# Other loads for the decay columns, and a new order for the first eight stages of a fused linear-attention and MLP kernel

## The chip, the cores and the metric

The kernel runs on one core of a Trainium2 chip. The metric is device time in microseconds (us) of one execution, and the kernel before has a median of 165.37 us over three runs (165.07 to 165.39). The engines are PE (TensorE), DVE (VectorE), ACT (ScalarE), POOL (GpSimd) and SP (SyncE). Each has its own instruction stream, runs it in order, and waits on semaphores. SP, ACT and POOL also issue DMAs, each on queues of its own: in the profile q1 carries SP's loads, q10 those of ACT, and q0 those of POOL.

## The reference, cut to what matters

Four batches, eight heads, 768 tokens, head size 48. Per token and head the output is the query times the state plus a bonus for the token itself, and the state then decays by `w` and takes in the new key and value. The result, 3072 tokens by 384, goes through two matrices with a leaky ReLU between them.

```python
for t in range(S):
    kt, vt, rt = k[:, :, t], v[:, :, t], r[:, :, t]
    cur = einsum('bhd,bhe->bhde', u[None] * kt, vt)
    y[:, :, t] = einsum('bhd,bhde->bhe', rt, state + cur)
    state = w[None, :, :, None] * state + einsum('bhd,bhe->bhde', kt, vt)
x = y.transpose(0, 2, 1, 3).reshape(3072, 384)
h = x @ w_in                      # 384 -> 2048
out = maximum(0.01 * h, h) @ w_out  # 2048 -> 384
```

## The kernel before, in words

The 768 tokens of a batch are cut into 6 chunks of 128, which makes 24 stages. In a stage, tables of powers of `w` scale r and k (`prep`, written P; P5.0 is the half with r of stage 5, P5.1 the half with k). PE turns the products so that the head dimension lies on partitions (`turn`, T), ACT copies them from PSUM to SBUF, and PE forms the 128 by 128 score blocks (`a_mm`, A). DVE masks these into `at` (`a_mask`, M), multiplies the turned halves for the bonus (`diag`, X, into `prod`), and scales v by the bonus (`prep2`, Q, into `vs`). PE forms the bonus sums and the state's new part (`kv_mm`, K), DVE updates the state (`state`, S), and PE sums the stage's output from `at`, `st` and `vs` (`y_part`, Y), which ACT copies to `xT`. Then come the first matrix (`g1` for one stage, G; `g1_pair` for two stages, J) and the second (`g2`, H; `g2_seven`, N).

Stages 0 to 7 turn on PE; later ones by DMA transposes. A planner does not decide the order. A string of step names, `ORDER`, is walked from left to right, and each step appends its instructions to the streams of its engines; waits follow from what each reads and writes. So the string sets the order on all engines at once, up to about 60 us of the run. Behind it a plain loop emits the remaining pairs of stages. A second string, `LOADS`, sets the order of POOL's first instructions, most of them DMA issues: `t` is a column of token numbers (iota), `tri` the causal mask, `id` the identity, `wi0` a quarter of the first matrix, `r3` r of stage 3.

r and k of stages 0 and 1 do not come through POOL: SP issues those of r, ACT those of k, behind the small rows of `w` and `u`. `decay_columns` (C) brings `w` and `w*u` from a row on one partition to columns, head by head, by matmuls with one output column each. Their results feed `wcol` (ACT, logarithm) and `wu` (DVE), and through them the decay table `wl` (`decay_table`, W) and the bonus sums of K. `fill` (F) is a matmul of ones with ones whose result nobody reads.

```python
FIRST, EARLY = 8, 2
add("sp", lambda: SP.dma_start(w_row[:, :], row(w)), W=["w_row"], dma="w")
```

Of the kernel before, what the change touches and what calls it, by code (L numbers as in the profile page):

```python
# [16 lines left out]
HD = H * D  # L17
E = 64
# [106 lines left out]
def bass_rwkv5_eagle__then__act_leaky_relu_kernel(  # L125
# [49 lines left out]
    wu_row = SB("wu_row", [1, HD])  # L175
# [127 lines left out]
    for name in LOADS.split():  # L303
# [16 lines left out]
    add("dve", lambda: V.tensor_tensor(wu_row[:, :], w_row[:, :], u_row[:, :], ALU.mult),  # L320
        R=["w_row", "u_row"], W=["wu_row"])
# [7 lines left out]
    add("dve", lambda: V.memset(wu[:, :, :], 0.0), W=["wu"])  # L329
    fill(EARLY)  # L330
# [89 lines left out]
    def turn(n, *halves):  # L420
        it, iq = n % NTP, n % NQK
        for half in halves or ((0, 1) if n == 0 else (1, 0)):
            ps_t, key = next_bank()

            def emit(half=half, ps_t=ps_t):
                for p in range(NP):
                    h0 = half * H + 2 * p
                    last = PE.matmul(ps_t[:, 128 * p:128 * p + 128],  # L428
                                     qk[iq][:, h0:h0 + 2, :].rearrange("p h e -> p (h e)"), ident[:, :],
                                     start=True, stop=True)  # L430
# [4 lines left out]
            add("act", lambda dst=dst, ps_t=ps_t: A.activation(dst, ps_t[:, :], AF.Copy),  # L435
                R=[key], W=[("tp", it, half)])
# [51 lines left out]
    def a_mask(n, *parts):  # L488
# [9 lines left out]
        for hh in parts or range(2):  # L498
            part = at_bank[n][hh][0][:, :].rearrange("p (m i) -> p m i", i=128)
            add("dve", lambda hh=hh, part=part: V.tensor_tensor(  # L500
                at[n % NAT][:, hh, :, :], part, mask[:, :].unsqueeze(1).to_broadcast([128, NP, 128]), ALU.mult),
                R=[at_bank[n][hh][1], "mask"], W=[("at", n % NAT, hh)])
# [30 lines left out]
    def decay_columns():  # L533
        ps_c, key_c = next_bank()

        def emit():
            for hh in range(2):
                for p in range(NP):
                    c0 = (2 * p + hh) * D
                    rows = slice(64 * hh, 64 * hh + D)  # L540
                    PE.matmul(ps_c[rows, p:p + 1], w_row[:, c0:c0 + D], one_row[:, 0:1], start=True, stop=True)
                    last = PE.matmul(ps_c[rows, NP + p:NP + p + 1], wu_row[:, c0:c0 + D], one_row16[:, 0:1],
                                     start=True, stop=True)
            return last

        add("pe", emit, R=["one_row", "one_row16", "w_row", "wu_row"], W=[key_c, "wcols"])
# [322 lines left out]
    steps = {"U": u_table, "V": u_cast, "P": prep, "Q": prep2, "B": bonuses, "O": g_sum, "N": lambda m, *step: g2_seven(m, step=step[0] if step else None), "b": skip_banks, "I": g2_store, "t": swapped_tables, "m": swapped_mask, "E": lambda n, *heads: diag_tile(n, heads or range(H)), "D": lambda n: diag_tile(n, None), "T": turn, "A": a_mm, "M": a_mask, "K": kv_mm, "R": carry, "S": state, "Y": y_part, "X": diag, "C": decay_columns, "W": decay_table, "w": load_wout, "F": fill, "Z": w_sum,  # L869
# [116 lines left out]
```

## Time and profile before

| what | value |
|---|---|
| median of three runs | 165.37 us |
| the profiled execution | 165.09 us |
| its span (first to last instruction) | 163.4 us |
| PE busy in the span | 156.3 us (96%) |
| DVE, ACT, POOL busy | 124.4, 126.4, 79.1 us |
| loads from memory | 20.45 MB read, 4.72 MB written |

The span is what the trace shows; the execution's own time has 1.7 us more around it. A busy PE may still run slowly: the duration of a matmul of known size tells its rate, and the busy share does not. In the tables of groups and in the timeline the columns are the start, the time, the engine, the line of the kernel, the operation, and output and inputs; a wait, with what ended it, stands in brackets at the end.

### The profile page before, as it was taken

The page shows a single profiled execution, that of the slowest core. Times are in us where ns is not written, and L with a number is a line of the kernel's source. Part 1 is how long each engine was busy: PE and PEld are TensorE (multiplying, and loading weights), DVE is VectorE, ACT ScalarE, POOL GpSimd, SP SyncE. Part 2 cuts the span into 40 slices and gives each one's busy share as a digit, 9 for nine tenths or more (in the row PEclk, how much of TensorE's full clock was granted, in tenths as well). Part 3 has the DMA queues.
Part 4 walks back from the last instruction along what each step waited for, and adds up shares of the span by engine and source line. Part 5 has one row for each costly group of instructions (what it writes and reads, how often), then busy time and mean ns, then how long its engine had stood idle before and what let it go on. Part 6 is the DMA issues. An engine that isn't in the chain of part 4 may idle for free.

```text
span 163.4 us, 5788 instructions
## 1 busy us (share of the span) xinstructions
PE 156.3 (96%) x2444; PEld 135.4 (83%) x2444; DVE 124.4 (76%) x264; ACT 126.4 (77%) x313; POOL 79.1 (48%) x106
## 2 busy tenths in 40 slices
PE   5688999999999999999999999999999999999993
PEld 3557888788667889889889899899898899898993
DVE  7498997859999299997988988689889467055353
ACT  3565889879467989999999989989899827829430
POOL 7999992999936991780870961910000000000000
PEclk9999999999999999999999999999999999999999
DMA  5999999999999999999999996998209103003033
GB/s 107 161 172 184 157 155 173 202 188 139 140 118 177 169 204 127 179 105 93 192 105 95 186 110 118 178 85 153 72 4 194 35 4 96 0 18 84 4 96 98
DMA packets 99710, 19.91 MB, mean 122 GB/s; under 512 B 92770, under 2 KB 99684, under 8 KB 99684
## 3 DMA queue, kind: packets, MB, share of 16 engines
q0 software_dynamic: 74768, 9.84, 93.8%
q1 hardware_dynamic: 22836, 9.31, 29.4%
q10 hardware_dynamic: 2080, 0.39, 1.3%
q8 instruction: 19, 0.31, 0.8%
q14 instruction: 7, 0.06, 0.1%
HBM read 20.45 MB, written 4.72 MB: 154 GB/s over the span
## 4 chain that ended last, share of the span: by engine, by line
PE 90%; DVE 4%; DMA 4%; SPq 1%; issue 1%; DVEq 0%
PE ps_all L647 38%; PE ps_all L741 29%; PE ps_all L602 7%; PE ps_all L664 6%; DMA out_sb<-in_r_dram 4%; PE ps_all L516 2%; PE ps_all L469 2%; PE ps_all L451 2%; PE ps_all L428 2%; DVE at L500 2%; DVE qk L367 1%; DVE vs L383 1%; PE ps_all L630 0%; PE ps_all L512 0%; DVE st L567 0%
## 5 line engine op out<-in xcount | busy, mean ns | idle before, releaser
L647 PE MATMUL ps_all<-xT,w_in_sb 128*128 128x256 bf16 x564 | 65.0, 273 | 0.0
L647 PEld LDWEIGHTS ps_all<-xT,w_in_sb 128*128 128x128 bf16 x564 | 54.3, 98 | 6.5
L653 ACT ACTIVATE gT<-ps_all 128x512 bf16<-128x512 f32 x94 | 52.5, 596 | 3.5 <-PE ps_all L647 1.2
L416 ACT ACTIVATE at<-ident,s_tok 128x128 bf16<-128x128 bf16 x120 | 38.2, 392 | 0.3 <-DVE s_tok L397 0.3
L238 POOL DMA_DIRECT2D rk_sb<-in_k_dram x15 | 13.9, 925 | 19.4 <-PE ps_all L647 19.4
L741 PE MATMUL ps_all<-tw,gs 128*128 128x192 bf16 x240 | 22.9, 246 | 0.0
L771 DVE TENSOR_TENSOR out_sb<-ps_all,snap 128x192 f32<-128x192 f32 x31 | 10.8, 355 | 15.0 <-PE ps_all L741 14.7
L741 PEld LDWEIGHTS ps_all<-tw,gs 128*128 128x128 bf16 x240 | 20.0, 98 | 0.0
L741 PE MATMUL ps_all<-w_out_sb,gT 128*128 128x192 bf16 x160 | 16.5, 246 | 0.0
L711 DVE TENSOR_TENSOR gs<-gT 128x1024 bf16<-128x1024 bf16 x20 | 13.6, 683 | 2.9 <-ACT gT L653 2.9
L238 POOL DMA_DIRECT2D v_sb<-in_v_dram x17 | 15.7, 942 | 0.0
L492 DVE CAST_PREDICATED at<-mask,ps_all 128x1024 bf16<-128x1024 uint16 x9 | 10.9, 1220 | 5.5 <-PE ps_all L469 3.1
L238 POOL DMA_DIRECT2D rk_sb<-in_r_dram x15 | 13.9, 932 | 0.4 <-issue 0.4
L749 ACT ACTIVATE snap<-ps_all 128x192 f32<-128x192 f32 x30 | 9.9, 330 | 5.5 <-PE ps_all L741 4.9
L617 ACT ACTIVATE xT<-ps_all 128x384 bf16<-128x384 f32 x24 | 11.0, 488 | 3.7 <-PE ps_all L602 3.4
L741 PEld LDWEIGHTS ps_all<-w_out_sb,gT 128*128 128x128 bf16 x160 | 13.0, 98 | 0.5
L602 PE MATMUL ps_all<-at,v_sb 128*32 128x128 bf16 x384 | 12.0, 224 | 0.8 <-DVE vs L383 0.8
L435 ACT ACTIVATE tp<-ps_all 128x512 bf16<-128x512 f32 x16 | 9.1, 595 | 3.7 <-PE ps_all L428 3.6
L500 DVE TENSOR_TENSOR at<-ps_all,mask 128x512 bf16<-128x512 f32 x16 | 10.6, 686 | 1.8 <-PE ps_all L451 1.7
L235 POOL DMA_DIRECT2D rk_sb<-in_k_dram x14 | 10.0, 746 | 3.0 <-PE ps_all L647 3.0
L602 PEld LDWEIGHTS ps_all<-at,v_sb 128*32 128x32 bf16 x384 | 9.1, 98 | 2.7 <-DVE vs L383 1.4
L235 POOL DMA_DIRECT2D v_sb<-in_v_dram x14 | 10.0, 745 | 2.7 <-PE ps_all L664 1.5
(94 smaller groups left out, 248.3 us busy)
## 6 DMA issues: line engine op xcount, KB each, us to landing
out_dram<-out_sb SPq DMA_DIRECT2D x15, 192.0 KB, 2.5
out_dram<-out_sb SPq DMA_DIRECT2D x18, 96.0 KB, 2.2
v_sb<-in_v_dram POOLq DMA_DIRECT2D x17, 96.0 KB, 6.1
w_in_sb<-in_moe_w_in_dram POOLq DMA_DIRECT2D x4, 384.0 KB, 7.2
w_out_sb<-in_moe_w_out_dram POOLq DMA_DIRECT2D x4, 384.0 KB, 10.1
rk_sb<-in_r_dram POOLq DMA_DIRECT2D x15, 96.0 KB, 5.9
rk_sb<-in_k_dram POOLq DMA_DIRECT2D x15, 96.0 KB, 6.0
rk_sb<-in_k_dram POOLq DMA_DIRECT2D x14, 48.0 KB, 4.9
```

Of the source, the lines that this page charges most:

```text
L235: add("pool", lambda to=to, of=of: G.dma_start(dst[to], src[of]), R=pace, W=[(which, slot, half)], dma=f"{which}{n}{half}")
L238: add("pool", lambda: G.dma_start(dst, src), R=pace, W=[(which, slot, 0), (which, slot, 1)], dma=f"{which}{n}")
L416: add("act", lambda h=h: A.activation(at[ia][:, h % 2, h // 2, :], ident[:, :], AF.Copy, scale=s_tok[n % 4][:, h:h + 1]), R=["ident", ("s" ...
L492: add("dve", lambda: V.copy_predicated(at[n % NAT][:, :, :, :].rearrange("p two m i -> p (two m) i"), (mask_s if swapped(n) else mask)[:, ...
L500: add("dve", lambda hh=hh, part=part: V.tensor_tensor(at[n % NAT][:, hh, :, :], part, mask[:, :].unsqueeze(1).to_broadcast([128, NP, 128]) ...
L602: last = PE.matmul(ps_y[32 * q:32 * q + 32, 128 * s:128 * s + 128], a, m, start=first_mm, stop=last_mm)
L617: add("act", lambda: A.activation(xT[m % NX][:, :, 128 * half:128 * half + 128], ps_y[:, 0:HD].rearrange("p (s t) -> p s t", t=128), AF.Copy),
L647: last = PE.matmul(ps_g[:, 256 * f:256 * f + 256], w_in_sb[:, s, 128 * fb:128 * fb + 128], xT[ix][:, s, :], start=s == 0, stop=s == NSL - 1)
L653: add("act", lambda: A.activation(gT[ig][:, 2 * j:2 * j + 2, :].rearrange("p f t -> p (f t)"), ps_g[:, :], AF.Prelu, alpha=0.01), R=[key], ...
L711: add("dve", lambda: V.tensor_tensor(x[i][:, :, :], a, b, op), R=keys, W=[("gs", m % 2, i)])
L741: done = PE.matmul(ps_o[:, 0:NH], lhs[:, s, :], rhs[:, s, :], start=first and s == 0, stop=s == HF - 1, skip_group_check=not (first and last))
L771: add("dve", lambda: V.tensor_tensor(out_sb[io][:, cols], ps_o[:, 0:NH], snap[i2][i][:, :], ALU.add), R=[key, ("snap", i2, i), *after], W= ...
```

## The change

1. **Columns.** `w` and `u` are loaded a second time, as [8, 48], one head per partition (`w_heads` on SP, `u_heads` on ACT). `wu_row` on one partition gives way to `wu_heads` on eight. `decay_columns` then needs four matmuls in place of sixteen: the [8, 48] tile is the stationary operand, and every second column of an 8 by 8 identity (`ident_f`, a copy in fp32) picks the heads.
2. **Loads on SP and ACT.** On SP the order becomes row of w, `w_heads`, r of stages 0 and 1, row of u. On ACT `u_heads` stands between k of stage 0 and k of stage 1.
3. **POOL.** The mask comes first, then v of stage 0, and the identity is made fifth and not seventh. The order of all loads in `LOADS` is another.
4. **Two new step kinds.** `c` masks a score half in two steps (ACT copies PSUM to SBUF, DVE multiplies in SBUF by the mask); it is used once, at stage 1. `d` turns a half with DVE, not ACT, copying it out of PSUM; it is used for one half each of stages 6 and 7.
5. **ORDER** is drawn anew from its first line to its last, with three fills in place of one.

```diff
-LOADS = """t r3 v0 r2 wi0 tri id k3 k2 v1 wi1 v3 v2 wi2 r6 k4 r4 r5 k5 v4 k6 v5 k7 wi3 v6 v7 r7"""
+LOADS = """tri v0 t wi0 id r2 k3 v1 r3 k2 v2 wi1 v3 wi2 r4 k4 k5 v4 k6 r6 r5 v5 k7 wi3 r7 v6 v7"""
 ORDER = """
-P0.0 P0.1 P1.0 C P1.1 T0.0 T0.1 F1 X0 W A0 w2 M0.0 K0 M0.1 T1.0 Q0 P2.0 T1.1 Y0 X1 A1 M1.1 T2.0 P2.1 S0 G0.0 K1 T2.1 M1.0 P3.1 Q1 Y1 T3.1 P3.0 S1 X2
+P0.0 P0.1 C F1 F1 P1.1 T0.0 T0.1 W P1.0 X0 A0 T1.0 M0.1 M0.0 K0 T1.1 F1 Q0 Y0 S0 P2.0 A1 X1 P3.1 M1.0 c1.1 T2.0 P3.0 T3.1 G0.0 P2.1 K1 w1 T2.1 Q1 S1
...
     add("sp", lambda: SP.dma_start(w_row[:, :], row(w)), W=["w_row"], dma="w")
+    add("sp", lambda: SP.dma_start(w_heads[:, :], w), W=["w_heads"], dma="w8")
+    load_first("r", 0)
+    load_first("r", 1)
     add("sp", lambda: SP.dma_start(u_row[:, :], row(u)), W=["u_row"], dma="u")
-    for n in range(2):
-        load_first("k", n)
-        load_first("r", n)
+    load_first("k", 0)
+    add("act", lambda: A.dma_start(u_heads[:, :], u), W=["u_heads"], dma="u8")
+    load_first("k", 1)
...
-    add("dve", lambda: V.tensor_tensor(wu_row[:, :], w_row[:, :], u_row[:, :], ALU.mult),
-        R=["w_row", "u_row"], W=["wu_row"])
...
+    add("dve", lambda: V.tensor_copy(ident_f[:, :], ident[0:H, 0:H]), R=["ident"], W=["ident_f"])
+    add("dve", lambda: V.tensor_tensor(wu_heads[:, :], w_heads[:, :], u_heads[:, :], ALU.mult),
+        R=["w_heads", "u_heads"], W=["wu_heads"])
...
-                for p in range(NP):
-                    c0 = (2 * p + hh) * D
-                    rows = slice(64 * hh, 64 * hh + D)
-                    PE.matmul(ps_c[rows, p:p + 1], w_row[:, c0:c0 + D], one_row[:, 0:1], start=True, stop=True)
-                    last = PE.matmul(ps_c[rows, NP + p:NP + p + 1], wu_row[:, c0:c0 + D], one_row16[:, 0:1],
-                                     start=True, stop=True)
+                rows = slice(64 * hh, 64 * hh + D)
+
+                def side(x):
+                    return x.rearrange("p (m two) -> p two m", two=2)[:, hh, :]
+
+                PE.matmul(ps_c[rows, 0:NP], w_heads[:, :], side(ident_f[:, :]), start=True, stop=True)
+                last = PE.matmul(ps_c[rows, NP:2 * NP], wu_heads[:, :], side(ident[0:H, 0:H]), start=True, stop=True)
...
+            if copied:
+                add("act", lambda hh=hh, part=part: A.activation(at[n % NAT][:, hh, :, :], part, AF.Copy),
+                    R=[at_bank[n][hh][1]], W=[("at", n % NAT, hh)])
+                add("dve", lambda hh=hh: V.tensor_tensor(
+                    at[n % NAT][:, hh, :, :], at[n % NAT][:, hh, :, :],
+                    mask[:, :].unsqueeze(1).to_broadcast([128, NP, 128]), ALU.mult),
+                    R=[("at", n % NAT, hh), "mask"], W=[("at", n % NAT, hh)])
+                continue
...
+                add("dve", lambda dst=dst, ps_t=ps_t: V.tensor_copy(dst, ps_t[:, :]), R=[key], W=[("tp", it, half)])
```

Three places show what the strings do to the streams. The line numbers of the changed kernel are a little higher: 428 becomes 435 (turn), 451 becomes 461 (scores), 512 and 516 become 530 and 534 (K), 602 becomes 621 (Y), 630 becomes 649 (G), 370 and 367 become 377 and 374 (P with r and with k), 500 becomes 518 (mask), 383 becomes 390 (Q), 567 becomes 586 (S of stage 0).

**POOL, its first instructions.** Before:

```order
L292 IOTA tcol 128x1
L238 DMA rk_sb<-in_r_dram 128x8x48
L238 DMA v_sb<-in_v_dram 128x8x48
L238 DMA rk_sb<-in_r_dram 128x8x48
L256 DMA w_in_sb<-in_moe_w_in_dram 128x3x512
L300 AFFINE_SELECT mask<-ones 128x128
L296 AFFINE_SELECT ident<-ones 128x128
```

After:

```order
L306 AFFINE_SELECT mask<-ones 128x128
L241 DMA v_sb<-in_v_dram 128x8x48
L298 IOTA tcol 128x1
L259 DMA w_in_sb<-in_moe_w_in_dram 128x3x512
L302 AFFINE_SELECT ident<-ones 128x128
L241 DMA rk_sb<-in_r_dram 128x8x48
L241 DMA rk_sb<-in_k_dram 128x8x48
```

The first load of POOL now stands behind the mask, which reads `ones`, a tile that DVE sets; and the first quarter of the first matrix is the second load and not the fourth.

**DVE, from P of stage 0 to Q of stage 1.** Before:

```order
L370 TENSOR_TENSOR qk<-out_sb,tab 128x8x48
L551 CAST wu<-ps_all 48x4 x2
L367 TENSOR_TENSOR qk<-out_sb,tab 128x8x48
L375 TENSOR_TENSOR prod<-tp 128x512
L500 TENSOR_TENSOR at<-ps_all,mask 128x512 x2
L383 TENSOR_TENSOR vs<-v_sb,ps_all 128x384
L370 TENSOR_TENSOR qk<-rk_sb,tab 128x8x48
L375 TENSOR_TENSOR prod<-tp 128x512
L500 TENSOR_TENSOR at<-ps_all,mask 128x512
L367 TENSOR_TENSOR qk<-rk_sb,tab 128x8x48
L567 TENSOR_TENSOR st<-ps_all,wl 128x384
L500 TENSOR_TENSOR at<-ps_all,mask 128x512
```

After:

```order
L382 TENSOR_TENSOR prod<-tp 128x512
L518 TENSOR_TENSOR at<-ps_all,mask 128x512 x2
L390 TENSOR_TENSOR vs<-v_sb,ps_all 128x384
L586 TENSOR_TENSOR st<-ps_all,wl 128x384
L377 TENSOR_TENSOR qk<-rk_sb,tab 128x8x48
L382 TENSOR_TENSOR prod<-tp 128x512
L374 TENSOR_TENSOR qk<-rk_sb,tab 128x8x48
L518 TENSOR_TENSOR at<-ps_all,mask 128x512
L513 TENSOR_TENSOR at<-at,mask 128x512
L377 TENSOR_TENSOR qk<-rk_sb,tab 128x8x48
L374 TENSOR_TENSOR qk<-rk_sb,tab 128x8x48
L390 TENSOR_TENSOR vs<-v_sb,ps_all 128x384
```

Ahead of the first `prod` the two copies to `wu` and k of stage 1 now stand ahead of r of stage 1. The state's update of stage 0 moves to the front, ahead of P2.0, and one of the two masks of stage 1 reads SBUF.

**PE, from A of stage 0 to Y of stage 1, without the rows of Y.** Before:

```order
L428 MATMUL ps_all<-ident,qk 128x128 x8
L284 MATMUL ps_all<-ones 128x512
L451 MATMUL ps_all<-tp 128x128 x8
L512 MATMUL ps_all<-wu,prod 128x2 x4
L516 MATMUL ps_all<-v_sb,qk 128x96 x4
...
L451 MATMUL ps_all<-tp 128x128 x8
L428 MATMUL ps_all<-ident,qk 128x128 x4
L630 MATMUL ps_all<-xT,w_in_sb 128x128 x12
L512 MATMUL ps_all<-wu,prod 128x2 x4
L516 MATMUL ps_all<-v_sb,qk 128x96 x4
L428 MATMUL ps_all<-ident,qk 128x128 x4
```

After:

```order
L461 MATMUL ps_all<-tp 128x128 x8
L435 MATMUL ps_all<-ident,qk 128x128 x4
L530 MATMUL ps_all<-wu,prod 128x2 x4
L534 MATMUL ps_all<-v_sb,qk 128x96 x4
L435 MATMUL ps_all<-ident,qk 128x128 x4
L290 MATMUL ps_all<-ones 128x512
...
L461 MATMUL ps_all<-tp 128x128 x8
L435 MATMUL ps_all<-ident,qk 128x128 x8
L649 MATMUL ps_all<-xT,w_in_sb 128x128 x12
L530 MATMUL ps_all<-wu,prod 128x2 x4
L534 MATMUL ps_all<-v_sb,qk 128x96 x4
L435 MATMUL ps_all<-ident,qk 128x128 x4
```

One half of T1 moves ahead of K0, a fill of one matmul moves from behind T0 to behind T1 (Y0 is what the dots stand for), and four matmuls of T3 join the four of T2 ahead of G0.

More of the change, by code (lines that the diff above doesn't have):

```diff
@@ L174, in bass_rwkv5_eagle__then__act_leaky_relu_kernel @@
     wcol = SB("wcol", [128, NP], FP32)
-    wu_row = SB("wu_row", [1, HD])
+    w_heads = SB("w_heads", [H, D], FP32)
+    u_heads = SB("u_heads", [H, D], FP32)
+    wu_heads = SB("wu_heads", [H, D])
+    ident_f = SB("ident_f", [H, H], FP32)
     u_row16 = SB("u_row16", [1, HD])
@@ L418, in diag_tile, with turn @@
                 R=["ident", ("s", n % 4)], W=[("at", ia, h % 2)])
-    def turn(n, *halves):
+    def turn(n, *halves, copier="act"):
         it, iq = n % NTP, n % NQK
@@ L486, in a_blocks, with a_mask @@
             W=[key for x in stages for _, key in at_bank[x]])
-    def a_mask(n, *parts):
+    def a_mask(n, *parts, copied=False):
         if n >= DIAG:
@@ L537, in emit @@
             for hh in range(2):
-                for p in range(NP):
-                    c0 = (2 * p + hh) * D
-                    rows = slice(64 * hh, 64 * hh + D)
-                    PE.matmul(ps_c[rows, p:p + 1], w_row[:, c0:c0 + D], one_row[:, 0:1], start=True, stop=True)
-                    last = PE.matmul(ps_c[rows, NP + p:NP + p + 1], wu_row[:, c0:c0 + D], one_row16[:, 0:1],
-                                     start=True, stop=True)
+                rows = slice(64 * hh, 64 * hh + D)
[3 more added lines that the diff above has]
+                last = PE.matmul(ps_c[rows, NP:2 * NP], wu_heads[:, :], side(ident[0:H, 0:H]), start=True, stop=True)
             return last
-        add("pe", emit, R=["one_row", "one_row16", "w_row", "wu_row"], W=[key_c, "wcols"])
+        add("pe", emit, R=["ident", "ident_f", "w_heads", "wu_heads"], W=[key_c, "wcols"])
         for hh in range(2):
@@ L867, in skip_banks @@
         taken[0] += n
-    steps = {"U": u_table, "V": u_cast, "P": prep, "Q": prep2, "B": bonuses, "O": g_sum, "N": lambda m, *step: g2_seven(m, step=step[0] if step else None), "b": skip_banks, "I": g2_store, "t": swapped_tables, "m": swapped_mask, "E": lambda n, *heads: diag_tile(n, heads or range(H)), "D": lambda n: diag_tile(n, None), "T": turn, "A": a_mm, "M": a_mask, "K": kv_mm, "R": carry, "S": state, "Y": y_part, "X": diag, "C": decay_columns, "W": decay_table, "w": load_wout, "F": fill, "Z": w_sum,
+    steps = {"c": lambda n, *parts: a_mask(n, *parts, copied=True), "d": lambda n, *halves: turn(n, *halves, copier="dve"),
+             "U": u_table, "V": u_cast, "P": prep, "Q": prep2, "B": bonuses, "O": g_sum, "N": lambda m, *step: g2_seven(m, step=step[0] if step else None), "b": skip_banks, "I": g2_store, "t": swapped_tables, "m": swapped_mask, "E": lambda n, *heads: diag_tile(n, heads or range(H)), "D": lambda n: diag_tile(n, None), "T": turn, "A": a_mm, "M": a_mask, "K": kv_mm, "R": carry, "S": state, "Y": y_part, "X": diag, "C": decay_columns, "W": decay_table, "w": load_wout, "F": fill, "Z": w_sum,
              "G": g1, "J": g1_pair, "H": g2, "L": load_paced,
```

18 lines of the change are left out of this document (10 added, 8 removed).

## The prediction

> **What bounds the kernel now.** First the page: PE's busy tenths in 40 slices, and the chain that ended last, by engine.
>
> ```profile
> PE   5688999999999999999999999999999999999993
> PE 90%; DVE 4%; DMA 4%; SPq 1%; issue 1%; DVEq 0%
> ```
>
> PE is full from the fifth slice to the last. An edit can gain only at the start, where PE idles or runs slowly, or by taking work off PE. PE's waits over the whole span (in total, times, longest) say where it idles; the two largest that matter here:
>
> ```profile
> PE ps_all L428 <- DVE qk L370: 1.6, 1, 1.6
> PE ps_all L602 <- DVE vs L383: 0.8, 2, 0.5
> ```
>
> The first is T0, the other two are Y0 and Y1; from Y1 (15.93 us) on, PE never waits. So the end moves by as much as the point moves at which PE is full with the same work behind it. I take the start of Y3 as that point: both orders have the same main steps ahead of it (T, A, K of stages 0 to 3, two G, three J, Y0 to Y2).
>
> Next PE's timeline, for its rate:
>
> ```profile
> 9.09 0.61 PE L451 MATMUL ps_all<-tp 48*128 48x128 bf16 x8 [0.33 <-ACT tp L435]
> 13.41 1.49 PE L630 MATMUL ps_all<-xT,w_in_sb 128*128 128x128 bf16 x12
> 14.70 0.29 PE L512 MATMUL ps_all<-wu,prod 128*128 128x2 bf16 x4
> 17.50 0.83 PE L630 MATMUL ps_all<-xT,w_in_sb 128*128 128x128 bf16 x12
> 22.11 0.24 PE L602 MATMUL ps_all<-at,v_sb 128*32 128x128 bf16 x4
> ```
>
> G0's twelve matmuls take 1.49 us, G1's 0.83. With 0.3 and 0.2 for the last one's own time, the step is (1.49 - 0.31)/11 = 0.107 us at 13.41 and 0.055 at 17.50. PE runs at half rate early on, and the steps inside these rows put the turn near 15. The row at 22.11 is Y3's first.
>
> The chain of waits (start, time) tells what released Y0 and Y1, and how long PE's steps are at full rate:
>
> ```profile
> 1.93 6.00 DMA out_sb<-in_r_dram
> 9.44 0.33 DVE prod L375
> 9.80 1.29 DVE at L500 x2
> 11.09 0.47 DVE vs L383
> 11.61 0.94 PE ps_all L602 x14
> 12.54 0.56 PE ps_all L451 x8
> 13.12 0.69 DVE at L500
> 13.82 0.26 DVE qk L367
> 14.08 0.47 DVE st L567
> 15.93 0.74 PE ps_all L602 x40
> 16.67 0.33 PE ps_all L428 x4
> 17.00 0.33 PE ps_all L451 x8
> 17.66 0.67 PE ps_all L630 x12
> 18.33 0.08 PE ps_all L512 x4
> 18.41 0.19 PE ps_all L516 x4
> ```
>
> Up to Y1 the bound is mostly DVE's queue. In DVE's timeline stand Q1, then a block of ten steps (S1, X2, M2, X3, Q2, Q3, M3, S2) from 16.06 to 21.97 without a gap:
>
> ```profile
> 15.33 0.55 DVE L383 TENSOR_TENSOR vs<-v_sb,ps_all 128x384 bf16<-128x384 bf16 x1
> 16.06 0.55 DVE L570 TENSOR_TENSOR sum_t<-ps_all,st 128x384 bf16<-128x384 f32 x1
> 21.37 0.68 DVE L500 TENSOR_TENSOR at<-ps_all,mask 128x512 bf16<-128x512 f32 x1
> 21.97 0.35 DVE L370 TENSOR_TENSOR qk<-rk_sb,tab 128x384 bf16<-128x384 bf16 x1
> ```
>
> The block is 21.97 - 16.06 = 5.91 us long and Y3 starts 0.14 behind it: Y3 too was released by DVE, just in time for PE.
>
> **The change, part by part.** *Columns by four matmuls.* C's first and last row on PE, and the step of DVE that T0 waits for:
>
> ```profile
> 4.19 0.32 PE L541 MATMUL ps_all<-one_row,w_row 1*48 1x1 f32 x2
> 5.55 0.17 PE L542 MATMUL ps_all<-one_row,wu_row 1*48 1x1 bf16 x1
> 6.62 0.56 DVE L370 TENSOR_TENSOR qk<-r_f,tab 128x384 bf16<-128x384 f32 x1 [1.69 <-DMA r_f<-in_r_dram]
> ```
>
> Sixteen matmuls take 5.72 - 4.19 = 1.5 us; four, at the same each, save 1.1. That is hidden: T0 waits for r of stage 0, which DVE gets at 6.62. DVE idles 1.69 us ahead of that, and the two small operations that C now needs fit in, if the identity is ready (below). I take 0; without that cover it would be the 1.1.
>
> *SP and ACT.* `w_heads` stands where u's row stood, so r of stages 0 and 1 is issued when it was. On ACT `u_heads` pushes k of stage 1 back by about one issue of a small load, and DVE wants it only behind P0.1 and `wu`. Both 0.
>
> *POOL's order.* Its first load was issued at 1.41. Now the mask stands ahead of it and waits for `ones`, whose first reader shows when they are there:
>
> ```profile
> 1.41 1.04 POOL L238 DMA_DIRECT2D rk_sb<-in_r_dram  x1 [0.38 <-issue]
> 4.92 0.34 POOL L300 TENSOR_SCALAR_AFFINE_SELECT mask<-ones 128x128 bf16<-128x128 bf16 x1
> 1.65 1.03 PE L284 MATMUL ps_all<-ones 128*128 128x512 bf16 x2 [1.65 <-DVE ones L276]
> ```
>
> So v of stage 0 is issued at 1.62 + 0.34, about 1.95 us: 0.5 later than POOL's first load so far. The identity follows two issues of about one microsecond and is made near 4.2, in time for C. The delay frees the DMA engines for r. First r of stage 0 (issue, then time to landing), then the packets of SP's queue q1 and POOL's q0 from 4 to 5 us:
>
> ```profile
> 1.46 0.43 SPq L220
> r_f<-in_r_dram SPq DMA_DIRECT2D x1, 192.0 KB, 5.0
> q1 hardware_dynamic: 630, 0.12, 87.5%
> q0 software_dynamic: 249, 0.02, 44.4%
> ```
>
> r of stage 0 lands at 6.46. If q0's packets come 0.5 us later, up to 200 of the roughly 1000 in a microsecond go to others ahead of its end: 0.2 us. The bounds are 0 (nothing passes to q1) and 0.35 (all that q0 did until then). I take 0.2, and shift the chain by it: T0 7.13, A0 8.89, masks of stage 0 from 9.60, Y0 11.41. That k of stage 1 now goes ahead of r of stage 1 on DVE only keeps `prod` from being later than that.
>
> *From Y0 to Q1.* On PE there now stand A1 (0.55), T2.0 and T3.1 (four steps, 0.43 each), G0 (twelve, 1.29) and K1 (0.5) behind Y0 (0.86 at half rate). That is 4.06: at half rate K1 ends at 15.47 and Q1 starts near 15.55. On DVE, by the chain's steps from 9.60: masks 1.21 + vs 0.47 + st 0.47 + P2.0 0.27 + prod 0.33 + P3.1 0.27 + mask 0.60 + the mask in SBUF 0.40 (unseen; between `prod`, its like in SBUF, and the PSUM mask's 0.60) + P3.0 and P2.1 0.54 = 4.56, so DVE is free at 14.16. At full rate from Y0's end (12.27) PE needs 0.33 + 0.33 + 0.33 + 0.67 + 0.27 = 1.93, and Q1 starts near 14.25. So far it started at 15.33.
>
> *From Q1 to Y3.* On DVE Q1 0.46, the ten steps 5.91, then 0.14: Y3 comes 6.51 behind Q1's start. PE takes as long: 22.11 - 15.93 less the moved T3.1 (0.33) is 5.85, from a Y1 that comes 0.6 behind Q1. Against 22.11 the gain is 15.60 less the start of Q1: 0.05 if PE stays slow up to 15, and 1.35 if it is fast from 12.3. Between these ends stands the moment at which PE speeds up. So far that came some 3.4 us after Y0's start, ahead of which PE stood still for about 0.5. The fill behind T1 (0.43 long) closes most of that gap, and the half of T1 ahead of K0 closes the one behind A0. A shorter gap lies between the row that has one and one with none, so I take the middle, 0.7.
>
> [...]
>
> *Behind Y3.* Two turned halves go from ACT to DVE, 0.6 us each. DVE has idle time there, in one stretch (near 33 us):
>
> ```profile
> DVE st L567 <- PE ps_all L516: 1.8, 1, 1.8
> ```
>
> Nothing there is on the path while PE has J's to run, which wait for no DVE work of later stages. I take 0; a loss of up to 0.6 (one step of DVE that PE then waits for) is in the range.
>
> *Sum.* 0.7 off the profiled execution's 165.09 is 164.4. That execution lies 0.28 below the median of the runs, so against 165.37 the forecast is **164.7 us**.
>
> **The rivals.**
>
> *Clock early.* PE is at full rate from Y0's end: 1.35 off, 164.0. For it: PE is then busy from A0 (8.9) on, but for one gap near 0.3. Against it: a gap of 0.33 (ahead of 9.09) and that ahead of Y0 were enough to hold it off before.
>
> *Clock as it was.* PE speeds up at 15 again: 0.05 off, 165.3. For it: T3.1 now stands ahead of G0 and K1, so PE at half rate, not DVE, releases Q1, and what DVE saves is idle.
>
> *r of stage 1 late (slower).* The first quarter of `w_in` is now the second load in q0 and not the fourth, and its packets are large. Alone (9.0 to 9.5 us) q0 moved 101 of them:
>
> ```profile
> q0 software_dynamic: 101, 0.10, 123.7%
> ```
>
> Its 384 take 1.9 us. If they come ahead of the tail of r of stage 1, that lands at up to 7.93 + 1.9 = 9.8. DVE takes P1.0 ahead of `prod`, the masks and Q0, so all these wait, and PE's T1.0 holds K0: masks from 10.7 and not 9.6, Y0 at 12.5, Q1 at 16.65, and the end 1.05 later than before: 166.4. It hurts from a landing of 8.3 on, and from 9.0 on it has eaten the 0.7. Against it: the 1024 packets of v come first in q0, and by 7.3 us q1 was all but done.
>
> [...]
>
> **How the numbers follow.** Forecast 0.47, clock early 0.13, clock as it was 0.20, r of stage 1 late 0.12, clock late 0.08. The range goes from just below the early clock to half-way into the slow cases, 163.9 to 165.9, and leaves out about 0.15. A measurement of this kernel tells 0.2% (0.33 us) from no change. Faster are the first two and a tenth of the third: 0.62; the same, the rest of the third: 0.18; slower, the last two: 0.20.
>
> **What would show it.** Right: DVE's P of stage 0 with r starts near 6.4; C ends on PE ahead of 5.8; Y0 starts near 11.4; the step of PE's matmuls goes from 0.107 to 0.055 between 12.5 and 14.5; Y3 starts near 21.4; PE waits for nothing behind Y1. Wrong: P1.0 waiting for r of stage 1 past 8.3; G0 wholly at 0.107 with Q1 past 15.5; a wait of PE between 22 and 60 us, where I cost the new order at nothing.

## The result, and the profile after

Twenty runs of the changed kernel have a median of 164.39 us (163.78 to 165.13), and twenty of the kernel before, beside them, 165.48 (165.04 to 166.33). The ratio is 0.9937, with a 95% interval of 0.9921 to 0.9953: the change takes 1.04 us off. The profiled execution is one of the longest of the twenty, 165.04 us with a span of 163.3, against 165.09 and 163.4 before. Read by itself it would say that nothing was won; where things stand inside it says more. Differences in the text are taken before rounding.

PE's busy tenths and the chain that ended last look as before:

```profile
PE   5689999999999999999999999999999999999993
PEclk9999999999999999999999999999999999999999
PE 89%; DVE 4%; DMA 3%; ACT 1%; issue 1%; SPq 0%; DVEq 0%
```

PE's waits over the whole span (in total, times, longest) do not:

```profile
PE ps_all L435 <- DVE qk L377: 0.8, 1, 0.8
PE ps_all L561 <- DVE wu_heads L335: 0.8, 1, 0.8
PE ps_all L461 <- ACT tp L443: 0.7, 1, 0.7
PE ps_all L877 <- ACT u_row L873: 0.3, 1, 0.3
PE ps_all L621 <- DVE vs L390: 0.3, 1, 0.3
PE ps_all L530 <- DVE st L586: 0.2, 1, 0.2
```

T0 waits half as long, since two fills stand in that time. A0 (the third) waits 0.7 and not 0.3. Y0's wait is gone; the one that is left is Y1's. Three waits are new: the second (C, for `wu_heads`), the fourth (U, the row of `u` spread over the partitions) and the last (K of stage 7).

PE's timeline shows the rate (start, time, what, and the idle time before it with what ended it):

```profile
8.96 0.61 PE L461 MATMUL ps_all<-tp 48*128 48x128 bf16 x8 [0.71 <-ACT tp L443]
10.76 0.63 PE L290 MATMUL ps_all<-ones 128*128 128x512 bf16 x1
11.42 0.30 PE L621 MATMUL ps_all<-at,v_sb 128*32 128x128 bf16 x4
12.83 0.83 PE L435 MATMUL ps_all<-ident,qk 128*128 128x128 bf16 x8
13.50 0.83 PE L649 MATMUL ps_all<-xT,w_in_sb 128*128 128x128 bf16 x12
20.03 0.33 PE L877 MATMUL ps_all<-u_row,one_row 1*128 1x384 bf16 x1 [0.31 <-ACT u_row L873]
38.58 0.25 PE L530 MATMUL ps_all<-wu,prod 128*128 128x2 bf16 x4 [0.24 <-DVE st L586]
```

The fill of T1 ends where Y0 starts, at 11.42. The twelve matmuls of G0 take 0.83 us, as G1's did before, and not 1.49: PE turns to full rate inside the row at 12.83. The trace's record of the clock has the turn at 13.32, against 14.96 before. Q1 (`vs`) starts at 14.64, 0.69 earlier than before; Y3 at 21.62, 0.48 earlier; the last matmul ends at 160.79, only 0.06 earlier. So this execution gains 0.69 us by Q1 and then loses 0.62 of it, 0.20 ahead of Y3 and 0.42 behind it.

A second profile of the same kernel (run e12_again, below) has the turn at 12.23, Q1 at 14.02, Y3 at 20.99, the last matmul's end at 160.06, and 164.32 us. The change's median lies near this one.

### The profile page after: what moved, and what is told of

The parts are those of the page before. It is cut to its first block, busy times and chain, and to the rows that moved or that the text cites. A ratio compares the mean times of both kernels' runs of the same rounds, so it can differ in the third digit from the quotient of the medians.

```text
span 163.3 us, 5756 instructions
## 1 busy us (share of the span) xinstructions
PE 156.0 (96%) x2428; PEld 133.6 (82%) x2428; DVE 126.6 (78%) x267; ACT 125.7 (77%) x312; POOL 79.2 (49%) x106
## 4 chain that ended last, share of the span: by engine, by line
PE 89%; DVE 4%; DMA 3%; ACT 1%; issue 1%; SPq 0%; DVEq 0%
PE ps_all L666 35%; PE ps_all L760 29%; PE ps_all L621 7%; PE ps_all L683 6%; DMA r_f<-in_r_dram 3%; PE ps_all L435 3%; PE ps_all L534 2%; PE ps_all L461 2%; PE ps_all L479 2%; PE ps_all L649 1%; DVE at L518 1%; ACT tp L443 1%; DVE vs L390 1%; DVE tp L446 0%; PE ps_all L530 0%
## 5 line engine op out<-in xcount | busy, mean ns | idle before, releaser
L241 POOL DMA_DIRECT2D v_sb<-in_v_dram x17 | 15.9, 941 | 0.0
L241 POOL DMA_DIRECT2D rk_sb<-in_r_dram x15 | 14.0, 936 | 0.0
L518 DVE TENSOR_TENSOR at<-ps_all,mask 128x512 bf16<-128x512 f32 x15 | 10.0, 686 | 0.9 <-PE ps_all L461 0.8
L683 PE MATMUL ps_all<-w_out_sb,gT 128*128 128x384 bf16 x64 | 10.7, 326 | 0.0
L238 POOL DMA_DIRECT2D rk_sb<-in_r_dram x14 | 10.4, 806 | 0.0
```

What stands on the lines that cost most here:

```text
L238: add("pool", lambda to=to, of=of: G.dma_start(dst[to], src[of]), R=pace, W=[(which, slot, half)], dma=f"{which}{n}{half}")
L241: add("pool", lambda: G.dma_start(dst, src), R=pace, W=[(which, slot, 0), (which, slot, 1)], dma=f"{which}{n}")
L518: add("dve", lambda hh=hh, part=part: V.tensor_tensor(at[n % NAT][:, hh, :, :], part, mask[:, :].unsqueeze(1).to_broadcast([128, NP, 128]) ...
L683: last = PE.matmul(ps_o[:, 0:HD], gT[ig][:, s, 128 * half:128 * half + 128], w_out_sb[:, s, :], start=s == 0, stop=s == NFB - 1)
```

## The experiments

In the diffs only the pieces of `ORDER` and `LOADS` that differ stand, against the changed kernel unless another is named. Ratios are to the kernel before, run beside each, with 95% intervals. All but one profile has a record of the turn to full rate ("turn"). The columns behind it are starts but for the last; all are us from the span's start in the one profiled run.

| run | median us | ratio | turn | Y0 | Q1 | Y3 | K7 | last matmul's end |
|---|---|---|---|---|---|---|---|---|
| before | 165.48 | 1 | 14.96 | 11.61 | 15.33 | 22.11 | 38.67 | 160.85 |
| after | 164.39 | 0.9937 (0.9921 to 0.9953) | 13.32 | 11.42 | 14.64 | 21.62 | 38.58 | 160.79 |
| e12_again | 164.47 | 0.9957 (0.9939 to 0.9976) | 12.23 | 11.09 | 14.02 | 20.99 | 37.85 | 160.06 |
| e1_cols | 165.68 | 1.0014 (0.9999 to 1.0029) | 14.45 | 11.75 | 15.47 | 22.25 | 38.82 | 160.99 |
| e2_nofill | 165.45 | 0.9989 (0.9971 to 1.0006) | 16.80 | 10.92 | 15.11 | 22.59 | 39.32 | 161.53 |
| e5_fill_t1 | 164.71 | 0.9952 (0.9933 to 0.9971) | 13.82 | 10.68 | 14.50 | 21.48 | 38.24 | 160.45 |
| e6_fill_c | 165.37 | 0.9992 (0.9975 to 1.0010) | none | 11.21 | 15.40 | 22.46 | 39.20 | 161.40 |
| e4_warm | 164.36 | 0.9933 (0.9913 to 0.9954) | 8.88 | 11.21 | 13.92 | 20.90 | 37.89 | 160.10 |
| e7_before_warm | 165.46 | 1.0008 (0.9992 to 1.0024) | 9.69 | 11.97 | 15.12 | 21.90 | 38.51 | 161.07 |
| e3_vearly | 165.05 | 0.9972 (0.9953 to 0.9991) | 14.22 | 11.16 | 14.94 | 21.66 | 38.58 | 160.79 |
| e8_best1 | 163.79 | 0.9908 (0.9892 to 0.9925) | 8.59 | 10.91 | 13.63 | 20.39 | 37.36 | 159.56 |
| e9_oldloads | 165.34 | 0.9988 (0.9973 to 1.0004) | 11.60 | 11.73 | 14.44 | 21.20 | 39.19 | 161.39 |
| e10_nocd | 163.93 | 0.9907 (0.9888 to 0.9925) | 9.14 | 11.00 | 13.93 | 20.73 | 37.48 | 159.68 |
| e11_best2 | 163.89 | 0.9903 (0.9885 to 0.9922) | 8.53 | 10.76 | 13.62 | 20.91 | 37.54 | 159.73 |

**The columns, and the loads on SP and ACT, alone.** The changed code with the two strings of before:

```diff
-LOADS = """tri v0 t wi0 id r2 k3 v1 ...
+LOADS = """t r3 v0 r2 wi0 tri id k3 ...
-P0.0 P0.1 C F1 F1 P1.1 T0.0 T0.1 W P1.0 ...
+P0.0 P0.1 P1.0 C P1.1 T0.0 T0.1 F1 X0 ...
```

> The kernel with the four matmuls and the [8, 48] loads, but with LOADS and ORDER of before. My theory (the columns are hidden behind r of stage 0, the gain is all in the order): within 0.2 us of before, ratio 0.999 to 1.001. DVE's first P with r still starts near 6.6, and Q1 near 15.3. Rival (the columns and the loads on SP and ACT carry part of the gain of 1.1 us): at least 0.4 us faster than before, ratio at most 0.9975, with Y0 earlier than 11.6. A loss is possible too, since the identity is made seventh here and C waits for it: C then ends near 6.5 and ACT's logarithm of its result near 6.9, still ahead of the first copy of T0 at 7.95, so nothing.

Measured 1.0014 (0.9999 to 1.0029): worth nothing, perhaps a little less. C needs four matmuls, but starts later: DVE makes `wu_heads` behind the copy of the identity, and the identity still stands seventh on POOL. PE's timeline:

```profile
5.88 0.33 PE L561 MATMUL ps_all<-ident_f,w_heads 8*48 8x4 f32 x4 [1.63 <-DVE wu_heads L335]
6.38 1.08 PE L435 MATMUL ps_all<-ident,qk 128*128 128x128 bf16 x8
```

T0 came at 6.38 against 7.33, because r of stage 0 landed 3.7 us after its issue here (5.0 before); Y0 came no earlier (11.75 against 11.61). What T0 gained was lost on DVE: there P of stage 1 with r stands ahead of `prod` and the masks, and it waited 1.37 us for its load and started at 8.16 (8.02 before).

**No fills.** Between T0 and Y0, and behind C, nothing but work:

```diff
-C F1 F1 P1.1
+C P1.1
-T1.1 F1 Q0
+T1.1 Q0
```

> The changed kernel without the three fills of ORDER (two behind C, one behind T1). My theory (the moment at which PE goes to full rate sets Q1, and the fills bring it forward): slower than the changed kernel by 0.2 to 0.6 us, ratio to before 0.995 to 0.998, and the step of PE's matmuls goes from 0.107 to 0.055 at 14.5 to 15 or later in the profiled execution. [...]

Measured 0.9989 (0.9971 to 1.0006): without three matmuls whose result nobody reads the gain is gone, though Y0 comes earlier (10.92). PE's timeline:

```profile
12.33 1.03 PE L435 MATMUL ps_all<-ident,qk 128*128 128x128 bf16 x8
13.16 1.48 PE L649 MATMUL ps_all<-xT,w_in_sb 128*128 128x128 bf16 x12
16.89 0.40 PE L435 MATMUL ps_all<-ident,qk 128*128 128x128 bf16 x4
```

G0 takes 1.48 us again and the turn comes at 16.80, later than before the change. PE at half rate then releases Q1: 4.19 us behind Y0, where the prediction had 4.14 for half rate.

**Which fill.** First T1's alone, then C's two alone:

```diff
-C F1 F1 P1.1
+C P1.1
```

> The changed kernel with only the fill behind T1 kept; the two behind C are taken out. Without all three the ratio to before was 0.9989, with all three 0.9937. The theory of the prediction (the fill that closes the gap ahead of Y0 brings the clock forward): most of the gain stays, ratio 0.993 to 0.996. [...]

```diff
-T1.1 F1 Q0
+T1.1 Q0
```

> The mirror of it: the two fills behind C are kept, the one behind T1 is taken out. The theory of the prediction: most of the gain is lost, ratio 0.997 to 0.9995. Rival (the fills behind C count): ratio 0.993 to 0.996.

T1's alone gives 0.9952 (0.9933 to 0.9971), C's alone 0.9992 (0.9975 to 1.0010). So one matmul of 0.43 us ahead of Y0 carries the gain, and the two behind C none that can be told. The place of the turn goes with it, in one profile of each: at 12.2 to 14.2 in the four profiles of the new order that have T1's fill and none behind T0 (after, e12_again, e5_fill_t1, e3_vearly), and past G0 in the two without. In the profile of C's alone, G0 is at half rate:

```profile
13.45 1.49 PE L649 MATMUL ps_all<-xT,w_in_sb 128*128 128x128 bf16 x12
```

**PE kept busy from the start.** Two fills behind the broadcast of the row of `w`, four behind C, two behind T0:

```diff
-C F1 F1 P1.1 T0.0 T0.1 W
+C F4 P1.1 T0.0 T0.1 F2 W
             R=["one_row", "w_row"], W=[key_w, "bc"])
+    fill(2)
```

> The changed kernel with fills in every gap of PE up to A0: two behind the broadcast of w's row, four and not two behind C, two behind T0. PE then has matmuls from 1.65 us on almost without a gap. [...] Rival (what PE does ahead of Y0 does not count, or Q1 is bound elsewhere): full rate between 11.5 and 15 as before, the same time as the changed kernel, ratio 0.993 to 0.995.

Measured 164.36 us, 0.9933 (0.9913 to 0.9954): the median of the change, not below it. All six runs lie within 0.25 us (164.35 to 164.60), where the change's twenty spread over 1.35. PE's timeline and waits:

```profile
5.44 1.89 PE L290 MATMUL ps_all<-ones 128*128 128x512 bf16 x4
7.12 1.06 PE L436 MATMUL ps_all<-ident,qk 128*128 128x128 bf16 x8
8.96 0.40 PE L462 MATMUL ps_all<-tp 48*128 48x128 bf16 x8
12.78 0.83 PE L650 MATMUL ps_all<-xT,w_in_sb 128*128 128x128 bf16 x12
```

```profile
PE ps_all L622 <- DVE vs L391: 1.0, 1, 1.0
```

A0 is already at full rate (0.40 for eight, 0.61 after), and PE waits 1.0 us for DVE ahead of Y0. From there DVE is the bound: Q1 comes 2.72 us behind Y0, where the prediction had 2.84 for full rate. This is the early end of the clock, and the change's median is no higher. But the four fills behind C also have a price: T0 starts behind the last of them, at 7.12, where with three fills (e8_best1, below) it starts at 6.82, though DVE started P of stage 0 with r later there (6.20 against 6.09).

**The same in the old order.** The kernel before with the same kind of fills:

```diff
-C P1.1 T0.0 T0.1 F1 X0
+C P1.1 F3 T0.0 T0.1 F2 X0
-P2.0 T1.1 Y0
+P2.0 T1.1 F1 Y0
             R=["one_row", "w_row"], W=[key_w, "bc"])
+    fill(2)
```

> The kernel before, its order and loads as they were, with fills in PE's gaps: two behind the broadcast of w's row, three behind C, two in place of one behind T0, one behind T1. The theory that in the old order Q1 is released by DVE's queue and not by PE's rate: full rate from 9 us or so on, but Q1 comes only 0.1 to 0.5 earlier than 15.33, the end 0.1 to 0.5 us (ratio 0.997 to 0.9995). Rival (the fills are the whole gain, the order is worth nothing): as fast as the changed kernel with fills, ratio 0.992 to 0.995.

Measured 1.0008 (0.9992 to 1.0024), where a small gain was expected. The turn came at 9.69, 5.3 us earlier than before, and the time is the same. PE's wait and DVE's timeline:

```profile
PE ps_all L603 <- DVE vs L384: 1.4, 2, 0.7
```

```profile
8.22 0.56 DVE L371 TENSOR_TENSOR qk<-out_sb,tab 128x384 bf16<-128x384 f32 x1 [0.68 <-DMA out_sb<-in_r_dram]
```

PE waits for Q0 and Q1 all the same, both on DVE. From Y0 to Q1 it took 0.57 us less than before (3.15 against 3.72), but Y0 came 0.36 later: the fills held T0 back to 7.88 (7.33 before), and P1.0, ahead of `prod` and the masks on DVE, waited for r of stage 1. What Q1 and Y3 had left of it, 0.2 us, was gone by the end. So these fills are worth nothing without the new order, and the new order nothing without its fills. What an early turn that delays nothing would give in the old order was not run.

**The two new waits.** V, ACT's copy of the row of `u` that U needs, moved ahead of Q1:

```diff
-w1 T2.1 Q1 S1
+w1 T2.1 V Q1 S1
-X3 Q2 V M3.0
+X3 Q2 M3.0
```

> The changed kernel with V (ACT's cast of u's row) moved ahead of Q1 and Y1, where ACT idles 0.42 us. In the changed kernel PE stands still 0.46 us ahead of U, which waits for that cast. My theory (PE is full around it, so each stall counts once): PE goes from J0.2 to U without a gap, and Y2 and Y3 come 0.35 to 0.45 us earlier relative to Y1. How much of it is left at the end is open: PE also stands still 0.40 us ahead of K7, released by DVE's update of the state of stage 6. If DVE's stretch ahead of that is bound by PE's T7 it moves along and the end gains 0.4 (ratio 0.990 to 0.992); if it is bound by DVE's own queue, the stall ahead of K7 grows by as much and the end stays (0.993 to 0.995).

Measured 0.9972 (0.9953 to 0.9991): above the change's own 0.9937, though U's wait is gone from the profile. The profiled run turned only at 14.22, so its Q1 (14.94) is late, and K of stage 7 stood at 38.58 as in the changed kernel, behind a wait of 0.19. With the turn free to fall anywhere, this comparison could not show 0.3 us. With the turn held early it could; here `t` and `m` (tables and mask for later stages, DVE) also go behind S6:

```diff
-C F1 F1 P1.1 T0.0 T0.1 W
+C F3 P1.1 T0.0 T0.1 F2 W
             R=["one_row", "w_row"], W=[key_w, "bc"])
+    fill(2)
-w1 T2.1 Q1 S1
+w1 T2.1 V Q1 S1
-X3 Q2 V M3.0
+X3 Q2 M3.0
-X7 t K6 A7 m M7.1
+X7 K6 A7 M7.1
-l10.37 S6 l11.21
+l10.37 S6 t m l11.21
```

> The changed kernel with fills in PE's gaps (two behind the broadcast, three behind C, two behind T0), V ahead of Q1, and the tables and the mask of the swapped stages (1.5 us of small DVE steps, now ahead of the masks of stage 7) moved behind the state's update of stage 6. With the fills alone the median was 164.36, the stalls of PE ahead of U and K7 0.46 and 0.40. Theory (each stall on a full PE counts once): both stalls are gone and the end is 0.6 to 0.9 us earlier, 163.5 to 163.8, ratio 0.988 to 0.990. Rival (DVE's queue binds from Q1 to Y3, as in the sum of the prediction, and behind it the loads): removing the stall ahead of U only moves the wait to Y2 or Y3, and the gain is 0.4 at most, ratio 0.990 to 0.993.

Measured 163.79 us (163.50 to 164.27), 0.9908 (0.9892 to 0.9925): below both kernels. It is clearly faster than the kernel before; against the changed kernel the medians differ by 0.6 us, and the intervals just overlap (0.9921 to 0.9953 there). PE's waits, all that are left behind its first instruction, then two rows of PE's timeline and two of DVE's:

```profile
PE ps_all L622 <- DVE vs L391: 0.8, 1, 0.8
PE ps_all L436 <- DVE sum_t L590: 0.2, 1, 0.2
```

```profile
5.45 1.46 PE L290 MATMUL ps_all<-ones 128*128 128x512 bf16 x3
6.82 1.07 PE L436 MATMUL ps_all<-ident,qk 128*128 128x128 bf16 x8
```

```profile
21.46 0.36 DVE L375 TENSOR_TENSOR qk<-rk_sb,tab 128x384 bf16<-128x384 bf16 x1 [0.64 <-DMA rk_sb<-in_k_dram]
21.74 0.55 DVE L590 TENSOR_TENSOR sum_t<-ps_all,st 128x384 bf16<-128x384 f32 x1
```

U's and K7's waits are gone. A new one stands near 22 us: T4.1 waits for S3 (`sum_t`), and that stands on DVE behind P5.1, which waits 0.64 for k of stage 5. The loads bind next.

Where the time went shows beside e4_warm, whose profile ends 0.54 later. 0.30 of that is there at Y0, where e8_best1 has one fill fewer ahead of T0. From Q1 to Y3 it gains 0.22 (6.76 against 6.98): U's wait. From K of stage 6 to K7 it gains 0.43 (3.98 against 4.41): K7's wait. From Y3 to K of stage 6 it loses 0.41 (12.99 against 12.58), the stall at T4.1, so behind Y3 nothing is left of it.

**The loads.** That kernel, with the POOL order of before:

```diff
-LOADS = """tri v0 t wi0 id r2 k3 v1 ...
+LOADS = """t r3 v0 r2 wi0 tri id k3 ...
```

> The kernel of the run before (fills in the gaps, V early, tables late; 163.79 us, ratio 0.9908) with the string LOADS of before, so that POOL issues r of stage 3 at 1.4 us and makes mask and identity sixth and seventh. With the clock opened early by the fills, what is left is the order of the loads. The prediction's step (POOL's later first load lets r of stage 0 land 0.2 us earlier): 0.2 us slower or a little more, ratio 0.992 to 0.9935, P of stage 0 with r starting near 6.6 and not 6.25. Rival one (landing of r moves with the run and not with POOL's order): the same, 0.990 to 0.992. Rival two (the late identity holds C, and PE's in-order queue with it, as the 1.6 us wait ahead of C in the columns-alone run showed): T0 is late by 0.3 us or more, ratio 0.993 to 0.996.

Measured 0.9988 (0.9973 to 1.0004), 1.3 us above e8_best1 by the ratios. The profiled runs end 1.8 us apart. DVE's waits up to 40 us, then PE's:

```profile
DVE ident_f L334 <- POOL ident L302: 1.1, 1, 1.1
DVE qk L375 <- DMA out_sb<-in_k_dram: 0.8, 1, 0.8
DVE qk L375 <- DMA rk_sb<-in_k_dram: 0.8, 1, 0.8
DVE qk L378 <- DMA rk_sb<-in_r_dram: 0.8, 1, 0.8
```

```profile
PE ps_all L436 <- DVE sum_t L590: 1.3, 1, 1.3
```

The identity is late and k of stage 1 is late: Y0, Q1 and Y3 each come 0.8 later. And r of stage 4 and k of stage 5 make S3 late, so that PE waits 1.3 us at T4.1, against 0.2 with the new loads: the other 1.0 us that is lost by the end. In this kernel the new `LOADS` is the third part without which there is no gain.

**The new step kinds.** e8_best1 with the plain forms in place of `c` and `d`:

```diff
-c1.1   d6.0   d7.0
+M1.1   T6.0   T7.0
```

> The same kernel with the two new step kinds undone: the second mask of stage 1 reads PSUM on DVE again, and both turned halves of stages 6 and 7 go through ACT. Theory (DVE's queue releases Q1 once the clock is open, and the mask in SBUF saves it 0.2 us there; the turned halves are off the path): Q1 comes 0.2 us later and the end is 0.1 to 0.3 us later, ratio 0.9915 to 0.993. Rival (the two kinds count for nothing): the same, 0.990 to 0.9915.

Measured 163.93 us, 0.9907 (0.9888 to 0.9925), as e8_best1. Q1 comes 2.93 behind Y0 and not 2.72, so `c` saves 0.2 us there; it doesn't reach the end.

**An earlier T0.** e8_best1 with k ahead of r in stage 0 and one fill fewer:

```diff
-P0.0 P0.1 C F3 P1.1 T0.0 T0.1 F2 W
+P0.1 P0.0 C F3 P1.1 T0.1 T0.0 F1 W
```

> The same kernel with k of stage 0 ahead of r of stage 0 on DVE and PE (P0.1 P0.0, T0.1 T0.0) and one fill, not two, behind T0. k of stage 0 landed at 4.0 and its table is ready at 5.8, r lands at 5.8 to 6.5. Theory (the chain from r's landing to A0 is DVE 0.48 for r, 0.48 for k, then PE and ACT; half of it can run ahead of the landing): A0, Y0 and Q1 0.3 to 0.5 us earlier and the end as much, 163.3 to 163.5, ratio 0.988 to 0.9895. Rival (r of stage 1 or the later loads bind next): less than 0.2, ratio 0.990 to 0.992.

Measured 163.89 us, 0.9903 (0.9885 to 0.9922): the same. Y0 comes 0.15 earlier, Q1 does not, and Y3 comes 0.5 later, with a wait of PE for the first matrix:

```profile
PE ps_all L667 <- DMA w_in_sb<-in_moe_w_in_dram: 0.2, 1, 0.2
```

**The changed kernel once more**, beside the last three:

> The changed kernel once more, for the spread and one more profiled execution. Theory (the end follows from the moment at which PE goes to full rate: 1.9 us behind Y0's start gave Q1 3.2 behind it and 165.04, never within Q1 gave 4.2 behind Y0): the times spread over 163.8 to 165.1 again, ratio 0.992 to 0.995, and in the profiled execution Q1 starts 2.7 to 4.2 us behind Y0, the more the later the full rate. Rival (the job, not the run, sets it): a median off by more than 0.4 from 164.4, with little spread.

Measured 164.47 us (164.28 to 165.38), 0.9957 (0.9939 to 0.9976). Its profiled run fell early, and PE's timeline shows the turn ahead of G0, inside this row:

```profile
11.96 0.51 PE L461 MATMUL ps_all<-tp 48*128 48x128 bf16 x8
```

The same program has Q1 0.63 earlier than in the first profile, Y3 0.63, the last matmul's end 0.73, and its time 0.72. Of the 0.63, 0.33 is there at Y0 (r of stage 0 landed 0.3 sooner), and 0.30 comes between Y0 and Q1, where the turn is 1.09 earlier.

## Why the prediction was right, and where its sizes were not

**What bounds.** Right. PE is full behind Y1 but for two stalls (0.31 at U and 0.24 at K7 by the rows of the waits), what is won at Q1 reaches the end less these, and the gain hangs on the point at which PE reaches full rate, as the two runs of the new order show that have G0 at half rate: 0.9989 in e2_nofill, 0.9992 in e6_fill_c. Of the signs that were named, C's end, Y0, the turn and Y3 came about as forecast in the first profile, and DVE's P of stage 0 with r did not (6.56; near 6.4 was forecast, 6.62 before). One sign of being wrong did come: a wait of PE between 22 and 60 us, at K7.

**The fill behind T1.** Right, and the main term. It was taken to close the gap ahead of Y0 and to bring the turn forward; e5_fill_t1 (0.9952, turn at 13.82) and e6_fill_c (0.9992, G0 at half rate) show that the gain goes with it, and with the fills behind C not as far as these runs can tell.

**The sum.** 0.7 off was forecast, 1.04 measured, and the forecast of 164.7 us lies 0.3 above the median. Two terms were mis-sized, in opposite directions:

- *The middle between the clock's ends.* Taken: Q1 at 14.9, 3.49 behind Y0, 0.7 off. The profiles have 3.22 and 2.93, nearer to the early end (2.84) than to the late one (4.14). With it Y0 comes up to 0.3 earlier than forecast (11.09 in e12_again). The end follows Q1 by about 146.1 us in both profiles, so the median of 164.39 wants Q1 near 14.05, as in the second (14.02, 164.32 us). The argument for the middle, that a shorter gap lies between a row with one and one with none, was the author's estimate and had no row behind it. e4_warm, with PE full from 4.2 us to its turn at 8.88, has the same median, less what its fourth fill cost at T0.
- *From Q1 to Y3.* Taken: 6.51, the work as before without T3.1. Measured: 6.98 in both profiles. The J ahead of U (six matmuls of 0.11 from 18.90) leaves PE free near 19.57, and U starts at 20.03, 0.46 late (the wait's row says 0.31, since it counts the last matmul's own time). ACT's timeline shows why:

```profile
18.83 0.60 ACT L672 ACTIVATE gT<-ps_all 128x512 bf16<-128x512 f32 x1 [0.76 <-PE ps_all L666]
19.45 0.52 ACT L873 ACTIVATE u_row<-u_row 1x384 bf16<-1x384 f32 x1
```

V now stood on ACT behind the copy of a J that itself waited for PE. With V moved Q1 to Y3 takes 6.76 in e8_best1 and 6.72 in e3_vearly. So U's wait is 0.2 to 0.3 of the 0.47 that the term was short; what the rest is was not found.

**Behind Y3.** Taken as 0, with up to 0.6 in the range; the first profile lost 0.42 there. K7 accounts for 0.39: it starts 16.96 us behind Y3, and 16.57 before the change, and the last matmul ends 122.2 us behind it in both. The chain of waits (start, time) names it:

```profile
33.74 0.70 DVE tp L446
...
34.98 0.15 DVE qexp_s L861
...
36.31 0.69 DVE at L518
37.38 0.68 DVE at L518
38.06 0.48 DVE st L586
```

The turned half `d7.0` (0.7) and 1.5 us of small steps of `t` and `m` (34.81 to 36.31) stand ahead of the masks of stage 7 and S6 (`st`), and the new order has S6 behind both masks. Before, S6 stood ahead of all of these, right behind the idle time of 1.8 us that the prediction counted on. DVE's timeline before:

```profile
35.16 0.56 DVE L567 TENSOR_TENSOR st<-ps_all,wl 128x384 bf16<-128x384 f32 x1 [1.85 <-PE ps_all L516]
```

The prediction did count the halves that go from ACT to DVE, and had missed `t`, `m` and the new place of S6. Its words "PE has J's to run" were wrong for K7, which stands in PE's order between J's and holds up those behind it. That U's wait cost about 0.2 to the end is borne out by e8_best1. That K7's cost 0.4 is not: with `t` and `m` moved its wait is gone, but T4.1's stall ahead of it takes as much, and the last matmul still ends 139.2 us behind Y3, as in the changed kernel (138.7 before). The two edits were not run apart with the turn held early, and e8_best1 against e4_warm (163.79 against 164.36) has the fill ahead of T0 in it too.

So some 0.6 us of the gain at Q1 was lost again by the end in the first profile, and the start gave more than was taken. That the sum came out close is in part luck, since these two errors go against each other.

**Columns: 0.** Right (e1_cols). In the changed kernel C ran from 5.04 to 5.40, behind a wait of 0.78 for `wu_heads`, and still ahead of T0.

**SP and ACT: 0 each.** The effect on k of stage 1 is as taken, the size is not. The issues on ACT's queue (start, time), then the rows of DVE for k and r of stage 1:

```profile
1.26 0.72 ACTq L278 DMA_DIRECT2D u_heads<-in_u_dram  x1
2.02 0.46 ACTq L223 DMA_DIRECT2D out_sb<-in_k_dram  x1
```

```profile
7.88 0.56 DVE L374 TENSOR_TENSOR qk<-out_sb,tab 128x384 bf16<-128x384 f32 x1
8.36 0.55 DVE L377 TENSOR_TENSOR qk<-out_sb,tab 128x384 bf16<-128x384 f32 x1
```

`u_heads` held the queue for 0.72 us, and k of stage 1 was issued at 2.02, where before it was at 1.26. It landed near 7.0, and DVE took it at 7.88 without a wait.

**POOL's order and the landing of r: 0.2.** The chain came as forecast: T0 at 7.18 (7.13 forecast), A0 at 8.96 (8.89), the masks at 9.62 (9.60), Y0 at 11.42 (11.41). The reason did not hold. The DMA issues between 0.5 and 4 us (KB each, us to landing), of the changed kernel and of e9_oldloads:

```profile
r_f<-in_r_dram SPq DMA_DIRECT2D x1, 192.0 KB, 4.9
out_sb<-in_k_dram ACTq DMA_DIRECT2D x1, 192.0 KB, 5.0
```

```profile
r_f<-in_r_dram SPq DMA_DIRECT2D x1, 192.0 KB, 3.8
out_sb<-in_k_dram ACTq DMA_DIRECT2D x1, 192.0 KB, 5.8
```

r lands earliest with the *old* order of POOL: 3.8 us here and 3.7 in e1_cols. With the change's order it took 3.9 to 4.9 in ten profiles (4.6 in e12_again), and 5.0 and 4.9 in the two with before's SP and ACT order (before, e7_before_warm). So what brings r forward, by half a microsecond in most profiles and by next to nothing in the first, is on SP's and ACT's side and not on POOL's. That it is the later k of stage 1 fits, and was not tried alone.

**From Y0 to Q1.** Right: forecast are 4.14 at half rate (15.55 less 11.41; measured 4.19 in e2_nofill) and 2.84 at full rate (14.25 less 11.41; measured 2.72 in e4_warm).

**The rivals.** *Clock early* is what the median came near to at Q1, and what it lost behind Q1 kept the time above that rival's 164.0. *Clock as it was* did not happen. *r of stage 1 late* did not: DVE took it at 8.36 (above) without a wait. *Clock late*, PE at half rate for longer than before, did happen where T1's fill is missing (16.80 in e2_nofill, 14.96 before), and cost the whole gain but no more. By how much it would be later was the author's estimate: the 1.84 us of e2_nofill is the most that a profile shows. The two profiles of the changed kernel show that the turn moves from run to run (13.32 and 12.23). That kernel's times spread over 1.35 us, those of e4_warm, where PE has no gap from 4.2 us to the turn, over 0.25. But with much the same fills the six runs of e8_best1 spread over 0.77 and the twelve of e7_before_warm over 0.99, so an early turn in the profile need not go with a small spread. In the profiles of before and after the trace's record of full rate lasts 150.19 us each, though it begins 1.64 earlier in the second; what sets its length was not shown.

**Open.** Why e3_vearly's median lies 0.6 above the change's, though it takes a wait away: its profiled run turned late, and whether its other runs did was not seen, as only one run of each was profiled.

## What to carry to other kernels

Where PE idles at the start, first find from the time of equal matmuls (0.107 against 0.055 us each here) when it reaches full rate, and then which engine releases the next step at each rate: here fills, order and loads had to come together. The runs without the fills (e2_nofill), without the loads (e9_oldloads) and with the fills alone (e7_before_warm) could not be told from no gain. Matmuls that nobody reads can fill the gaps, but count what stands behind them on PE: one too many held back the next step by 0.3 us. When a stall is taken away, look for the next one before the gain is booked: here a new stall took all that one of them gave back. And walk each wait that an order cuts, down to what stands queued ahead of it on the other engines, as far as the order reaches.

## What the runs showed that I had not expected

- One matmul of 0.43 us ahead of Y0 went with a turn 3.0 us earlier: 16.80 without any fill, 13.82 with it alone, one profile each.
- The page's row of the granted clock (PEclk) reads full from the first slice, also over the 13 us in which PE's matmuls run at half rate. The trace's record of the clock begins only at the turn, so what comes ahead of it is counted as full. The time of equal matmuls (0.107 against 0.055 us each) tells it.
- A [8, 48] load of 1.5 KB took 0.72 us to issue on ACT's queue, more than the 0.46 of the 192 KB load behind it, and more than the 0.29 of its like on SP (`w_heads`).
- Two executions of one program differ by 0.72 us in time (165.04 and 164.32), and 0.63 of that is there by Q1, at 14 us, half of it from the landing of one load.
